# A last half query tile shared by two head pairs, and the k of some groups transposed by TensorE

## The chip, the core and the metric

The kernel runs on one core of a Trainium2 chip. The metric is the device time of one execution in microseconds (us). Before the change it is 247.95 us, the median of three runs (247.35 to 249.12).

## What is computed

Blockwise causal attention for 8 batches of 8 heads (576 tokens, head size 64), then a layer on its output: two matrices, the larger of the two results for each element, and a third matrix.

```
scores = scale * np.matmul(q, k.transpose(0, 1, 3, 2))
mask = block_i >= block_j            # blocks of 64 positions
attn = softmax(np.where(mask, scores, -1e9))
x = np.matmul(attn, v)               # then (B, S, H * D) as (4608, 512)
h1 = x @ w1                          # (4608, 1024)
h2 = x @ w2
out = np.maximum(h1, h2) @ w_out     # (4608, 512)
```

Inputs and output are float32; products run in bfloat16 with float32 sums.

## The kernel before

**Tiling.** A *pair* p (0 to 31, four to a batch) is two heads that lie one above the other on the 128 partitions of `qT` and `kT`. A *group* g (0 to 15, `NG`) is two pairs, p = 2g and 2g + 1. The 576 queries of a pair are four tiles of 128 (t = 0 to 3) and one of 64 (t = 4, `NCH - 1`). Keys lie in five chunks c in the same way.

**Getting q and k in.** `load_qk` fetches a group's q and k by one request each of 576 KB on SP's queue (after a small Pool memset that holds the request until the buffer is free); `cast` makes them bfloat16 on Pool; `transposes` turns them with 18 TensorE transposes into two PSUM tiles (`ps_m`), which VectorE and ScalarE copy to `qT` or `kT`. q takes this way in all groups. For k, `by_dma` says from g = 6 on (`T_DMA`) that it comes otherwise: `load_blocks` issues four smaller requests from Pool that cast on the way, and `transpose_blocks` issues two DMA transposes on SP's queue. `t_pair` runs the transposes of the next group, q's in even steps and k's in odd ones; `pad_keys` then copies a piece of k on Pool.

**Attention.** `tile_0`, `tile_1` and `tile_2` put a pair's scores (TensorE, `scores` and `corner_scores`, on 64 rows of the array each, for the two heads) into two PSUM tiles `ps_s`; ScalarE takes exp into `aT`; Pool's memsets cut the masked corners (`mask`). Two steps later (`LAG`) `av` multiplies them with v: `aT` is the stationary operand, v with a column of ones the moving one (65 columns), so that the last column is the sum of the row. For query tile t it takes t + 1 matmuls a head. `av` is called twice a pair, for t = 0, 1 and for t = 2, 3, 4; for t = 4 it takes 128 columns of `aT`, 64 of which belong to no query (the padding `APAD`). VectorE takes reciprocals and multiplies into `xp`, bfloat16, three buffers of a pool (`xpool`), each for a group. `xp` is transposed into `xT` by TensorE (`x_out`) for groups 0 to 3 and 15, and for the others by two DMA transposes on SP's queue (`x_dma`).

**The layer.** Its matmuls are generators (`h_unit`, `product` and others) which `fill(n)` advances by n matmuls of weight between the attention parts. A maximum is rewritten with a difference matrix (`d_sb`, `m_sb`), and products of the blocks are combined from sums. They use the same four PSUM banks (`ps_m`) as `av` and the transposes.

**Order.** The order on every engine is the order of the calls (`manual_schedule`). After a start written out by hand, a loop over g = 3 to 15 does for each of its two pairs: `fill`, `av` of the pair two steps back in its two calls with a short `fill` between them, the DMA transposes that are due, `t_pair`, the scores of two tiles, the copies out, the exps, and `pool_work`, which issues Pool's later loads (q and k of group g + 3, casts for g + 2, v of the next batch but one in pieces by `load_v`, k's blocks). What is left of the group's fill comes at its end. After the loop, pairs 30 and 31 get their `av`, then `x_out(15)`, and the rest of the layer runs.

Of the kernel before, what the change touches and what calls it, by code (L numbers as in the profile page):

```python
# [8 lines left out]
FP32 = mybir.dt.float32  # L9
BF16 = mybir.dt.bfloat16  # L10
# [4 lines left out]
def kernel(  # L15
# [10 lines left out]
    nc = tc.nc  # L26

    B, H, S, D = q.shape
    P = 128
    BLK = 64  # L30
    HP = H // 2
# [12 lines left out]
    RPP = S // NP  # L44
    NG = NPAIR // 2
# [4 lines left out]

    CB = [0, 448, 768, 960, 1024]
    AW = 1600
    APAD = 64
    NCH = 5


# [3 lines left out]
    def a_col(p, c, t):  # L60
        if p >= HP:
            return CB[c] + t * P
        late = t * P >= QCUT
        return t * P + {
            0: 384 - QCUT if late else 0, 1: 704 - QCUT if late else 256 - P,
            2: 1024 - QCUT, 3: 1408 - 3 * P, 4: 1344 - 4 * P,
        }[c]
# [12 lines left out]
    wpool = ctx.enter_context(tc.tile_pool(name="wpool", bufs=1))  # L80
    ring = ctx.enter_context(tc.tile_pool(name="ring", bufs=1))
    small = ctx.enter_context(tc.tile_pool(name="small", bufs=4))
    xpool = ctx.enter_context(tc.tile_pool(name="xp", bufs=3))
    raw = ctx.enter_context(tc.tile_pool(name="raw", bufs=3))
    wraw = ctx.enter_context(tc.tile_pool(name="wraw", bufs=4))
    qkn = ctx.enter_context(tc.tile_pool(name="qkn", bufs=2))
    g_pool = ctx.enter_context(tc.tile_pool(name="g", bufs=2))
    y_pool = ctx.enter_context(tc.tile_pool(name="y", bufs=6))
    ps_s = ctx.enter_context(tc.tile_pool(name="ps_s", bufs=2, space=bass.MemoryType.PSUM))
    ps_m = ctx.enter_context(tc.tile_pool(name="ps_m", bufs=4, space=bass.MemoryType.PSUM))  # L90
# [1 line left out]
    ctx.enter_context(tc.manual_schedule())  # L92


    NV, NA, NT = 3, 4, 4
    qT_r = [ring.tile([P, S], BF16, name=f"qT{r}") for r in range(NT)]
    kz_r = [ring.tile([P, 3 * BLK], BF16, name=f"kz{r}") for r in range(NT)]
    kT_r = [ring.tile([P, S], BF16, name=f"kT{r}") for r in range(NT)]
    vv_r = [ring.tile([P, NCH, H, D + 1], BF16, name=f"vv{r}") for r in range(NV)]
    aT_r = [ring.tile([P, 2, AW + APAD], BF16, name=f"aT{r}") for r in range(NA)]  # L100
    xT = ring.tile([P, NDM, NTOK + BLK], BF16, name="xT")
    d_sb = wpool.tile([P, NDM, d_ff], BF16, name="d_sb")
    bT_sb = wpool.tile([P, NFF, d_model], BF16, name="bT_sb")
# [6 lines left out]
    qk_n = {}  # L110
    dve, pool, act = nc.vector.tensor_copy, nc.gpsimd.tensor_copy, nc.scalar.copy

    def load_qk(g, queues, gated=False):
        b, u = divmod(g, GPB)
        for nm, src, queue in (("q", q, queues[0]), ("k", k, queues[1])):
            if queue is None or by_dma(nm, g):
                continue
            raws[nm, g] = t = raw.tile([P, 2, RPP * D], FP32, name=f"{nm}raw")
            if gated:
                nc.gpsimd.memset(t[:, 0, :1], 0.0)  # L120
            queue.dma_start(
                out=t[:],
                in_=src[b, 4 * u:4 * u + 4].rearrange(
                    "(s h) (p t) d -> (h p) s (t d)", h=2, t=RPP),
            )

    T_DMA = {nm: 6 for nm in "k"}
    blk_n = {}

    def by_dma(nm, g):  # L130
        return g >= T_DMA.get(nm, NG)

    def load_blocks(nm, g):
        b, u = divmod(g, GPB)
        blk_n[nm, g] = n = raw.tile([P, S // BLK, 2, D], BF16, name=f"{nm}b", tag=f"{nm}raw")
        for h in range(2):
            for s in range(2):
                nc.gpsimd.dma_start(  # L138
                    out=n[h * BLK:(h + 1) * BLK, :, s],
                    in_=(q if nm == "q" else k)[b, 4 * u + 2 * s + h].rearrange(  # L140
                        "(j p) d -> p j d", p=BLK),
                )
# [10 lines left out]
    def cast(nm, g, parts):  # L153
        if by_dma(nm, g):
            return
        t = raws[nm, g].rearrange("p s (t d) -> p t s d", d=D)
        if (nm, g) not in qk_n:
            qk_n[nm, g] = qkn.tile([P, RPP, 2, D], BF16, name=f"{nm}n")
        n = qk_n[nm, g]
        for copy, j0, j1 in parts:  # L160
            copy(out=n[:, j0:j1], in_=t[:, j0:j1])  # L161

    def load_v(b, c):
        rows = min(P, S - c * P)
        nc.gpsimd.dma_start(  # L165
            out=vv_r[b % NV][P - rows:, c, :, :D],
            in_=v[b, :, c * P:c * P + rows, :].rearrange("h p d -> p h d"),
        )
# [7 lines left out]
    for j in range(d_ff // WB):  # L176
        row, n = (1, j) if j < 3 else (3, 0)
# [17 lines left out]
    def load_wo(i):  # L195
        ds = slice(i * WH, (i + 1) * WH)
        nc.gpsimd.dma_start(out=wo_sb[:, :, ds], in_=wor[:, :, ds])
# [13 lines left out]
    for r in range(NV):  # L211
        nc.vector.memset(vv_r[r][:, :, :, D:D + 1], 1.0)
        nc.vector.memset(vv_r[r][:BLK, NCH - 1, :, :], 0.0)
    for r in range(NA):
        nc.vector.memset(aT_r[r][:, :, AW:], 0.0)
    for r in range(NT):
        nc.vector.memset(kz_r[r][:, BLK:2 * BLK], 0.0)
    cast("q", 0, ((dve, 0, 7), (pool, 7, RPP)))
# [276 lines left out]
    def fill(n):  # L495
        while n > 0:
            if not current:
                k = next((k for k, t in enumerate(todo) if t[2] <= done_tokens[0]), None)
                if k is None:
                    return max(0, n)  # L500
                current.append(todo.pop(k))
            t = current[0]
            next(t[1])
            n -= t[3]
            t[0] -= 1
            if not t[0]:
                current.pop()
        return 0
# [8 lines left out]
    xps = {}  # L517
# [68 lines left out]
    def burst_q1(p):  # L586
        burst(p, ((0, QCUT, 320), (1, QCUT, 192)), 384)

    def burst_q2(p):
        burst(p, ((1, 448, P), (2, QCUT, 320), (4, 512, BLK)), 896)  # L590

    def burst_q3(p):
        burst(p, ((3, 384, 192),), 1408)
# [11 lines left out]
    def tile_0(p):  # L605
        u = ps_s.tile([P, 2, 512], FP32, name="ps_s", tag="s")
        scores(p, u, 0, 0, 0, 512)
        return lambda: (exp(p, u, 512, 0), mask(p, 0))

    def tile_1(p):  # L610
        u = ps_s.tile([P, 2, 512], FP32, name="ps_s", tag="s")
        scores(p, u, 0, 0, 512, 64)
        scores(p, u, 64, 1, 128, 448)
        return lambda: (exp(p, u, 512, 512), mask(p, 576))
# [17 lines left out]
    def region(*tiles):  # L632
        for out in tiles:
            out()

    def av(p, ts):
        b, hp = divmod(p, HP)
        vv = vv_r[b % NV]
        a = aT_r[p % NA]
        n = len(ts)  # L640
        h0 = hp // 2 * 4 + hp % 2
        if p % 2 == 0 and ts[0] == 0:
            xps[p // 2] = xpool.tile([P, 2, NCH, 2, D], BF16, name="xp")
        xp = xps[p // 2]
        po = ps_m.tile([P, n, 2, D + 1], FP32, name="ps_o", tag="m")
        n_mm = 2 * sum(t + 1 for t in ts)
        mm = 0
        for gi, t in enumerate(ts):
            for hh in range(2):
                for c in range(t + 1):  # L650
                    a0 = a_col(p, c, t)
                    nc.tensor.matmul(  # L652
                        po[:, gi, hh, :], a[:, hh, a0:a0 + P], vv[:, c, h0 + 2 * hh, :],
                        start=(mm == 0), stop=(mm == n_mm - 1),
                    )
                    mm += 1
        rec = small.tile([P, 3, 2, 1], FP32, name="rec")
        nc.vector.reciprocal(rec[:, :n, :, 0], po[:, :, :, D])  # L658
        nc.vector.tensor_mul(  # L659
            xp[:, :, ts[0]:ts[0] + n, p % 2].rearrange("q s t d -> q t s d"), po[:, :, :, :D],  # L660
            rec[:, :n].to_broadcast([P, n, 2, D]),
        )

    def x_by_dma(g):
        return BY_DMA <= g < NG - 1
# [48 lines left out]
    def pool_work(s):  # L714
        g, i = divmod(s, 2)
        if s == 4:
            load_qk(4, (SP, SP), gated=True)
        elif s == 5:
            load_qk(5, (SP, SP), gated=True)
            cast("q", 4, ((pool, 0, RPP),))  # L720
            cast("k", 4, ((pool, 0, RPP),))
        else:
            if i == 1 and g + 3 < NG:
                load_qk(g + 3, (SP, SP), gated=True)
            if i == 1 and g + 2 < NG:
                cast("q", g + 2, ((pool, 0, RPP),))
                cast("k", g + 2, ((pool, 0, RPP),))
            nb, j = divmod(s + 2, HP)
            if nb < B:
                for c in ((0, 1), (2, 3, 4), (), ())[j]:  # L730
                    load_v(nb, c)
            for nm in "qk":
                if i == 1 and g + 3 < NG and by_dma(nm, g + 3):
                    load_blocks(nm, g + 3)
# [12 lines left out]
    def av_with(p, n):  # L747
        av(p, [0, 1])
        fill(n)
        av(p, [2, 3, 4])  # L750

    LOW = (0, -(-QCUT // RPP))
    HIGH = (LOW[1], NP)
# [55 lines left out]
    burst_q1(2)  # L809
    transposes("q", 2, (dve, act))()  # L810
    burst_q2(2)
    av(0, [2, 3, 4])
    burst_q3(2)
    masks_q(2)
    cast("k", 2, ((pool, 0, RPP),))
    load_wo(0)
    load_wo(1)
    av(1, [2, 3, 4])
    burst_q1(3)
    burst_q2(3)  # L820
    av(2, [2, 3, 4])
    transposes("k", 2, (dve, act))()
    burst_q3(3)
    masks_q(3)
# [6 lines left out]
    diff_w(1)  # L831
    fill(2)
    outs = tile_0(4), tile_1(4)
    av(3, [2, 3, 4])
    region(*outs)
    fill(2)
    diff_w(2)
# [10 lines left out]
    n = fill_of(GPB)  # L848
# [10 lines left out]
    for g in range(GPB + 1, NG):  # L859
        a, b = 2 * g, 2 * g + 1  # L860
# [3 lines left out]
        n, new = fill_of(g), done_tokens[0]  # L864
# [72 lines left out]
```

## Time and profile before

The profiled execution took 247.61 us, with a span of 245.8 us from its first to its last instruction. PE is TensorE's matmuls, PEld its weight loads (which overlap the matmuls), DVE is VectorE, ACT ScalarE, POOL GpSimd, SP the queue engine. "Idle" is time in which the engine waited just before such an instruction.

| what | count | mean ns | idle before it, us |
|---|---|---|---|
| weights for attention times v, 128x128 (L652) | 960 | 98 | 6.9 |
| products of the layer, 128x256, `sums` and `bT_sb` (L390) | 216 | 273 | 0.0 |
| exp of 128x1024 (ACT, L568) | 92 | 1023 | 31.1 |
| reciprocal of 4 columns (DVE, L658) | 32 | 177 | 1.8 |
| reciprocal of 6 columns (DVE, L658) | 32 | 192 | 5.0 |
| cast of q, 128x1152 (POOL, L161) | 14 | 1160 | 0.6 |
| Pool's DMA issue for k's blocks (L138) | 40 | 765 | 0.0 |
| Pool's DMA issue for v (L165) | 40 | 857 | 1.1 |

| request | queue | count | KB each | median us to landing |
|---|---|---|---|---|
| q | SP | 16 | 576 | 6.0 |
| k, large | SP | 5 | 576 | 7.4 |
| k, blocks | POOL | 40 | 72 | 6.8 |
| v | POOL | 32 | 128 | 7.3 |
| DMA transposes of k | SP | 20 | | 6.5 |
| DMA transposes of xp | SP | 22 | | 5.4 |

How to read it: a matmul's length is its time through the array, and matmuls follow one another before the earlier one is out, so what one costs is the distance between two starts. In a row of the groups by shape, "128*128" is the part of the array that is used, rows by columns; then come output and input shapes, the count, the busy time, the mean length and the idle time before.

### The profile page before, as it was taken

What the parts mean: (1) busy time and instruction counts of PE and PEld (TensorE: products, weight loads), DVE (VectorE), ACT (ScalarE), POOL (GpSimd) and SP (SyncE); (2) the same over time, 40 slices, a digit from 0 to 9 for tenths busy, and PEclk for the clock granted to TensorE, in tenths of its full rate; (3) what the DMA queues carried; (4) which work ended last, traced back from release to release, by engine and by line L of the source; (5) the groups of instructions that cost most, each with busy time, mean ns of one, the idle gap of its engine ahead of it and who ended that gap; (6) DMA issues with size and microseconds to landing.
All of it is one profiled execution on the core that took longest, in us unless ns stands there. A gap on an engine that the chain in (4) does not pass through costs nothing.

```text
span 245.8 us, 7595 instructions
## 1 busy us (share of the span) xinstructions
PE 234.4 (95%) x3093; PEld 167.3 (68%) x3109; DVE 185.4 (75%) x395; ACT 143.8 (58%) x200; POOL 129.6 (53%) x294
## 2 busy tenths in 40 slices
PE   7689899999999999999999999999999999999993
PEld 2347666688865886588558755875587578567782
DVE  4976989999677958795879587957785788526573
ACT  2888871677677748673867386748673730462200
POOL 1996952669959584948593859485621210010000
PEclk9999999999999999999999999999999999999998
DMA  6999999579999999999999999999994321301125
GB/s 233 318 206 306 231 278 195 172 137 188 153 196 180 168 163 222 184 201 183 244 227 130 208 164 272 122 223 193 134 138 97 100 39 45 131 0 43 47 86 172
DMA packets 108867, 41.33 MB, mean 168 GB/s; under 512 B 89248, under 2 KB 102688, under 8 KB 108832
## 3 DMA queue, kind: packets, MB, share of 16 engines
q0 software_dynamic: 65952, 11.87, 69.4%
q1 hardware_dynamic: 42464, 28.32, 51.7%
q10 hardware_dynamic: 416, 0.66, 0.8%
q8 instruction: 24, 0.39, 0.7%
q14 instruction: 11, 0.09, 0.1%
HBM read 34.60 MB, written 9.44 MB: 179 GB/s over the span
## 4 chain that ended last, share of the span: by engine, by line
PE 87%; DVE 7%; ACT 4%; issue 1%; ACTq 0%
PE ps_p L390 35%; PE ps_h L244 24%; PE ps_o L652 11%; PE ps_s L544 9%; PE ps_w L514 3%; ACT aT L568 3%; PE ps_qT L525 2%; DVE sums L358 2%; DVE sums L364 1%; DVE g L252 1%; DVE m_sb L277 1%; PE ps_s L562 1%; PE ps_xe L690 1%; PE ps_bT L261 1%; DVE qT L533 1%
## 5 line engine op out<-in xcount | busy, mean ns | idle before, releaser
L568 ACT ACTIVATE aT<-ps_s 128x1024 bf16<-128x1024 f32 (+2 forms) x100 | 95.7, 994 | 32.1 <-PE ps_s L544 24.0
L244 PE MATMUL ps_h<-xT,d_sb 128*128 128x512 bf16 (+3 forms) x307 | 68.0, 357 | 1.0 <-DVE d_sb L191 0.3
L573 POOL MEMSET aT<- 64x128 bf16 x124 | 21.8, 200 | 52.8 <-ACT aT L568 51.9
L244 PEld LDWEIGHTS <-d_sb 128*128 128x128 bf16 x320 | 29.7, 98 | 26.7 <-issue 2.2
L652 PEld LDWEIGHTS <-aT 128*128 128x128 bf16 x960 | 37.2, 98 | 6.9 <-issue 0.8
L652 PE MATMUL ps_o<-vv,aT 128*128 128x65 bf16 x960 | 39.8, 194 | 0.3 <-DVE xp L659 0.3
L250 ACT ACTIVATE g<-ps_h 128x512 bf16<-128x512 f32 (+1 forms) x40 | 23.3, 587 | 23.3 <-PE ps_h L244 22.3
L165 POOL DMA_DIRECT2D vv<-in_v_dram x40 | 33.9, 857 | 1.1 <-issue 0.9
L252 DVE TENSOR_SCALAR g<-ps_h 128x512 bf16<-128x512 f32 (+2 forms) x40 | 23.6, 594 | 13.1 <-PE ps_h L244 12.8
L659 DVE TENSOR_TENSOR xp<-ps_o,rec 128x256 bf16<-128x256 f32 (+1 forms) x64 | 31.4, 491 | 2.2
L544 PE MATMUL ps_s<-qT,kT 64*128 64x64 bf16 (+6 forms) x344 | 31.3, 280 | 1.8 <-ACT kT L533 0.7
L390 PE MATMUL ps_p<-sums,bT_sb 128*128 128x256 bf16 x216 | 32.8, 273 | 0.0
L390 PEld LDWEIGHTS <-bT_sb 128*128 128x128 bf16 x288 | 27.5, 98 | 4.5 <-issue 1.4
L138 POOL DMA_DIRECT2D kb<-in_k_dram x40 | 29.5, 765 | 0.0
L533 ACT COPY qT<-ps_qT 128x576 bf16<-128x576 bf16 (+1 forms) x17 | 10.3, 614 | 23.2 <-PE ps_qT L525 23.2
L390 PEld LDWEIGHTS <-g 128*128 128x128 bf16 x220 | 19.8, 98 | 4.8 <-issue 2.8
L390 PE MATMUL ps_p<-wo_sb,g 128*128 128x256 bf16 (+1 forms) x148 | 22.7, 270 | 0.0
L161 POOL CAST qn<-qraw 128x1152 bf16<-128x1152 f32 (+1 forms) x16 | 17.1, 1067 | 5.1 <-DMA qraw<-in_q_dram 5.1
L544 PEld LDWEIGHTS <-kT 64*128 64x128 bf16 x344 | 12.2, 94 | 10.5 <-issue 5.1
L658 DVE RECIPROCAL rec<-ps_o 128x4 f32<-128x4 f32 (+1 forms) x64 | 11.8, 184 | 6.8 <-PE ps_o L652 6.8
L236 POOL COPY g<-g 128x512 bf16<-128x512 bf16 x8 | 5.9, 733 | 20.6 <-ACT g L250 20.3
L364 DVE TENSOR_TENSOR bT_sb<-g 128x1024 bf16<-128x1024 bf16 x18 | 12.4, 688 | 5.4 <-ACT g L250 4.8
(90 smaller groups left out, 326.1 us busy)
## 6 DMA issues: line engine op xcount, KB each, us to landing
qraw<-in_q_dram SPq DMA_DIRECT2D x16, 576.0 KB, 6.0
out_dram<-y SPq DMA_DIRECT2D x35, 256.0 KB, 3.9
vv<-in_v_dram POOLq DMA_DIRECT2D x32, 128.0 KB, 7.3
kraw<-in_k_dram SPq DMA_DIRECT2D x5, 576.0 KB, 7.4
kb<-in_k_dram POOLq DMA_DIRECT2D x40, 72.0 KB, 6.8
w1raw<-in_moe_w_dram POOLq DMA_DIRECT2D x4, 512.0 KB, 8.8
xT<-in_moe_w_dram POOLq DMA_DIRECT2D x4, 256.0 KB, 9.2
wo_sb<-in_moe_w_out_dram POOLq DMA_DIRECT2D x2, 512.0 KB, 10.9
```

Source lines behind the costliest of these rows:

```text
L138: nc.gpsimd.dma_start(out=n[h * BLK:(h + 1) * BLK, :, s], in_=(q if nm == "q" else k)[b, 4 * u + 2 * s + h].rearrange("(j p) d -> p j d", ...
L161: copy(out=n[:, j0:j1], in_=t[:, j0:j1])
L165: nc.gpsimd.dma_start(out=vv_r[b % NV][P - rows:, c, :, :D], in_=v[b, :, c * P:c * P + rows, :].rearrange("h p d -> p h d"),)
L244: nc.tensor.matmul(pt[:, :w], d_sb[:, c, f * P:(f + 1) * P], xT[:, c, t0:t0 + w], start=(c == 0), stop=(c == NDM - 1),)
L250: nc.scalar.activation(out=g[:, f, m:m + w], in_=pt[:, :w], func=AF.Relu)
L252: nc.vector.tensor_scalar_max(g[:, f, m:m + w], pt[:, :w], 0.0)
L390: nc.tensor.matmul(pt[:, q0:q0 + w], lhs[c][:, s * P:(s + 1) * P], rhs[c][:, m:m + w], start=(c == 0 and q0 == 0), stop=(c == 5 and q0 + w ...
L544: nc.tensor.matmul(ps[:, hh, col:col + w], kT[r, k0:k0 + P], qT[r, q0:q0 + w], start=True, stop=True,)
L568: nc.scalar.activation(out=aT_r[p % NA][:, :, a0:a0 + w], in_=ps[:, :, :w], func=AF.Exp, scale=scale,)
L573: (eng or nc.gpsimd).memset(aT_r[p % NA][BLK:, :, a0:a0 + BLK], 0.0)
L652: nc.tensor.matmul(po[:, gi, hh, :], a[:, hh, a0:a0 + P], vv[:, c, h0 + 2 * hh, :], start=(mm == 0), stop=(mm == n_mm - 1),)
L659: nc.vector.tensor_mul(xp[:, :, ts[0]:ts[0] + n, p % 2].rearrange("q s t d -> q t s d"), po[:, :, :, :D], rec[:, :n].to_broadcast([P, n, 2 ...
```

## The change

1. `av` for an even pair covers t = 0 to 3 alone. For an odd pair its second call covers t = 2, 3 and then t = 4 of both pairs of the group (`rest`): 64 columns of `aT` as the stationary operand, so that one head's output lies on the lower and the other's on the upper 64 partitions of the PSUM tile, the two heads alternating. The number of matmuls stays. VectorE multiplies these two halves by two instructions of 64 partitions each into the lower 64 partitions of `xp`.
2. `xp` becomes a ring of two fixed buffers (three before), whose upper half of tile 4 is set to zero at the start. The padding of `aT` and its memsets are gone.
3. `by_dma` now holds for odd groups alone: k of groups 6, 8, 10, 12 and 14 comes by `load_qk`, `cast` and `transposes`; for groups 8 to 14 the cast goes to a buffer of its own (`klate`). Groups 7, 9, 11, 13 and 15 keep Pool's blocks and the DMA transposes.
4. `pool_work` issues v's five chunks as 3, 1, 1 and 0 over four steps (2, 3, 0, 0 before).

```
     def by_dma(nm, g):
-        return g >= T_DMA.get(nm, NG)
+        return g >= T_DMA.get(nm, NG) and g % 2 > 0
...
         if (nm, g) not in qk_n:
-            qk_n[nm, g] = qkn.tile([P, RPP, 2, D], BF16, name=f"{nm}n")
+            if nm == "k" and g > T_DMA["k"]:
+                qk_n[nm, g] = klate.tile([P, RPP, 2, D], BF16, name="kl")
+            else:
+                qk_n[nm, g] = qkn.tile([P, RPP, 2, D], BF16, name=f"{nm}n")
...
     def av(p, ts):
...
+            xps[g] = xp_r[g % NX]
+        xp = xps[g]
+        rest = p % 2 and ts[0] > 0
+        n = 4 + 2 * rest
+        po = ps_m.tile([P, n, D + 1], FP32, name="ps_o", tag="m")
+        parts = [(po[:, 2 * gi + hh, :], p, hh, c, t, P)
+                 for gi, t in enumerate(ts) for hh in range(2) for c in range(t + 1)]
+        if rest:
+            parts += [(po[hh * BLK:(hh + 1) * BLK, 4 + i, :], p - 1 + i, hh, c, NCH - 1, BLK)
+                      for i in range(2) for c in range(NCH) for hh in range(2)]
+        for mm, (o, pp, hh, c, t, w) in enumerate(parts):
+            a0 = a_col(pp, c, t)
+            h0 = pp % HP // 2 * 4 + pp % 2
+            nc.tensor.matmul(
+                o, aT_r[pp % NA][:, hh, a0:a0 + w], vv[:, c, h0 + 2 * hh, :],
+                start=(mm == 0), stop=(mm >= len(parts) - 1 - rest),
+            )
+        rec = small.tile([P, 6, 1], FP32, name="rec")
+        nc.vector.reciprocal(rec[:, :n, 0], po[:, :, D])
         nc.vector.tensor_mul(
...
+            po[:, :4, :D].rearrange("q (t s) d -> q t s d", s=2),
+            rec[:, :4].rearrange("q (t s) d -> q t s d", s=2).to_broadcast([P, 2, 2, D]),
         )
+        if rest:
+            for s in range(2):
+                r = slice(s * BLK, (s + 1) * BLK)
+                nc.vector.tensor_mul(
+                    xp[:BLK, s, NCH - 1], po[r, 4:, :D], rec[r, 4:].to_broadcast([BLK, 2, D]))
...
-                for c in ((0, 1), (2, 3, 4), (), ())[j]:
+                for c in ((0, 1, 2), (3,), (4,), ())[j]:
                     load_v(nb, c)
...
-        av(p, [2, 3, 4])
+        av(p, [2, 3])
```

More of the change, by code (lines that the diff above doesn't have):

```diff
@@ L52 @@
     AW = 1600
-    APAD = 64
     NCH = 5
@@ L82 @@
     small = ctx.enter_context(tc.tile_pool(name="small", bufs=4))
-    xpool = ctx.enter_context(tc.tile_pool(name="xp", bufs=3))
     raw = ctx.enter_context(tc.tile_pool(name="raw", bufs=3))
@@ L86 @@
     qkn = ctx.enter_context(tc.tile_pool(name="qkn", bufs=2))
+    klate = ctx.enter_context(tc.tile_pool(name="kl", bufs=1))
     g_pool = ctx.enter_context(tc.tile_pool(name="g", bufs=2))
@@ L92 @@
     ctx.enter_context(tc.manual_schedule())
-    NV, NA, NT = 3, 4, 4
+    NV, NA, NT, NX = 3, 4, 4, 2
     qT_r = [ring.tile([P, S], BF16, name=f"qT{r}") for r in range(NT)]
@@ L99 @@
     vv_r = [ring.tile([P, NCH, H, D + 1], BF16, name=f"vv{r}") for r in range(NV)]
-    aT_r = [ring.tile([P, 2, AW + APAD], BF16, name=f"aT{r}") for r in range(NA)]
+    aT_r = [ring.tile([P, 2, AW], BF16, name=f"aT{r}") for r in range(NA)]
+    xp_r = [ring.tile([P, 2, NCH, 2, D], BF16, name=f"xp{r}") for r in range(NX)]
     xT = ring.tile([P, NDM, NTOK + BLK], BF16, name="xT")
@@ L125, in load_qk @@
             )
-    T_DMA = {nm: 6 for nm in "k"}
+    T_DMA = {"k": 6}
     blk_n = {}
     def by_dma(nm, g):
-        return g >= T_DMA.get(nm, NG)
+        return g >= T_DMA.get(nm, NG) and g % 2 > 0
     def load_blocks(nm, g):
@@ L213 @@
         nc.vector.memset(vv_r[r][:BLK, NCH - 1, :, :], 0.0)
-    for r in range(NA):
-        nc.vector.memset(aT_r[r][:, :, AW:], 0.0)
+    for r in range(NX):
+        nc.vector.memset(xp_r[r][BLK:, :, NCH - 1], 0.0)
     for r in range(NT):
@@ L637, in av @@
         b, hp = divmod(p, HP)
+        g = p // 2
         vv = vv_r[b % NV]
-        a = aT_r[p % NA]
-        n = len(ts)
-        h0 = hp // 2 * 4 + hp % 2
         if p % 2 == 0 and ts[0] == 0:
[L643 to L656, printed above, removed]
@@ L657, in av @@
-        rec = small.tile([P, 3, 2, 1], FP32, name="rec")
-        nc.vector.reciprocal(rec[:, :n, :, 0], po[:, :, :, D])
+            xps[g] = xp_r[g % NX]
[8 more added lines that the diff above has]
+                      for i in range(2) for c in range(NCH) for hh in range(2)]
@@ L659, in av @@
+        for mm, (o, pp, hh, c, t, w) in enumerate(parts):
[7 more added lines that the diff above has]
+        nc.vector.reciprocal(rec[:, :n, 0], po[:, :, D])
         nc.vector.tensor_mul(
-            xp[:, :, ts[0]:ts[0] + n, p % 2].rearrange("q s t d -> q t s d"), po[:, :, :, :D],
@@ L661, in av @@
-            rec[:, :n].to_broadcast([P, n, 2, D]),
-        )
+            xp[:, :, ts[0]:ts[0] + 2, p % 2].rearrange("q s t d -> q t s d"),
+            po[:, :4, :D].rearrange("q (t s) d -> q t s d", s=2),
+            rec[:, :4].rearrange("q (t s) d -> q t s d", s=2).to_broadcast([P, 2, 2, D]),
+        )
+        if rest:
[3 more added lines that the diff above has]
+                    xp[:BLK, s, NCH - 1], po[r, 4:, :D], rec[r, 4:].to_broadcast([BLK, 2, D]))
@@ L811 @@
     burst_q2(2)
-    av(0, [2, 3, 4])
+    av(0, [2, 3])
     burst_q3(2)
@@ L817 @@
     load_wo(1)
-    av(1, [2, 3, 4])
+    av(1, [2, 3])
     burst_q1(3)
     burst_q2(3)
-    av(2, [2, 3, 4])
+    av(2, [2, 3])
     transposes("k", 2, (dve, act))()
@@ L833 @@
     outs = tile_0(4), tile_1(4)
-    av(3, [2, 3, 4])
+    av(3, [2, 3])
     region(*outs)
```

## Prediction

> **What bounds the kernel now.** I read the page's busy table first, then the chain of waits in order of time, the busy time by stretch, the waits of each engine, the timeline of one group, and the groups by shape.
>
> The busy table and the head of the chain, then busy time by stretch (length, then busy us and instructions of PE, PEld, DVE, ACT, POOL, then clock, DMA share, GB/s):
>
> ```profile
> PE 234.4 (95%) x3093; PEld 167.3 (68%) x3109; DVE 185.4 (75%) x395; ACT 143.8 (58%) x200; POOL 129.6 (53%) x294
> ...
> PE 87%; DVE 7%; ACT 4%; issue 1%; ACTq 0%
> ```
>
> ```profile
> 24.00:34.00 10.00, 8.67 (x155) 6.66 (x151) 9.60 (x20) 8.88 (x12) 8.74 (x20) 1.00 1.32 250
> 34.00:52.00 18.00, 17.16 (x258) 12.94 (x256) 17.16 (x39) 7.99 (x12) 7.46 (x18) 1.00 1.20 205
> 60.00:200.00 140.00, 139.33 (x1870) 98.34 (x1879) 106.59 (x221) 93.42 (x127) 87.49 (x209) 1.00 1.57 174
> ```
>
> From 60 us on TensorE is busy 139.33 of 140 us at full clock, and the list of PE's waits in that stretch is empty: nothing there makes TensorE wait for a DMA, for Pool, for VectorE. The stage ends when TensorE has issued its list, so an edit there is worth what it adds to or takes from that list, and nothing else unless it makes a new wait. Before 52 us VectorE matters too: it is busy 9.60 of 10 us, then 17.16 of 18, and the chain runs through it:
>
> ```profile
> 45.05 1.03 DVE sums L358 x2
> 46.54 0.42 DVE xp L659
> 47.33 1.12 DVE sums L358
> 48.59 0.57 DVE xp L659
> 49.56 0.66 PE ps_M L272 x6
> ```
>
> From 49.56 us on it is TensorE's almost without a break. What Pool and the DMA queues carry is off the path: the only late wait for k's transposed blocks is Pool's own, 1.1 us in two places.
>
> ```profile
> POOL kz L551 <- DMA kT<-kb: 1.1, 2, 0.7
> ```
>
> **The prices on TensorE**, from the timeline of one even step (start, length, engine, what). A length ends with the last matmul's pipeline, so a pitch is (length - one matmul) / (count - 1).
>
> ```profile
> 100.70 1.90 PE L244 MATMUL ps_h<-xT,d_sb 128*128 128x512 bf16 x8
> ...
> 103.27 0.89 PE L652 MATMUL ps_o<-vv,aT 128*128 128x65 bf16 x24
> ...
> 104.08 0.44 PE L525 MATMUL ps_qT<-ident,qn 64*128 64x64 bf16 x18
> ...
> 104.36 0.22 PE L562 MATMUL ps_s<-qT,kz 64*128 64x64 bf16 x4
> ...
> 104.42 0.57 PE L544 MATMUL ps_s<-qT,kT 64*128 64x320 bf16 x6
> ...
> 104.92 0.39 PE L390 MATMUL ps_p<-wo_sb,g 128*128 128x256 bf16 x2
> ```
>
> ```profile
> L652 PE MATMUL ps_o<-vv,aT 128*128 128x65 bf16 x960 | 39.8, 194 | 0.3 <-DVE xp L659 0.3
> L659 DVE TENSOR_TENSOR xp<-ps_o,rec 128x384 bf16<-128x384 f32 x32 | 17.9, 558 | 1.1
> L659 DVE TENSOR_TENSOR xp<-ps_o,rec 128x256 bf16<-128x256 f32 x32 | 13.6, 424 | 1.1
> L533 DVE COPY qT<-ps_qT 128x576 bf16<-128x576 bf16 x15 | 11.2, 749 | 0.2 <-PE ps_qT L525 0.2
> L533 ACT COPY qT<-ps_qT 128x576 bf16<-128x576 bf16 x15 | 9.6, 639 | 23.2 <-PE ps_qT L525 23.2
> ```
>
> An attention matmul (128x65, whole array) costs (0.89 - 0.194) / 23 = 30.3 ns. Eighteen transposes on half arrays take from 104.08 to 104.36, 0.28 us less the 0.01 of the first one's late start, so 0.27 us: two, one on each half of the rows, pass in about 30 ns. Going from the whole array to half arrays costs: the last attention matmul starts at 103.27 + 0.70 = 103.97, the first transpose at 104.08, so 0.11 - 0.03 = 0.08 to 0.09 us. Going back: the 320-to-512 column scores end at 104.99, their last 512-column pair started 0.38 earlier at 104.61, the next product starts at 104.92: 0.31, of which a 512-column matmul takes (1.90 - 0.38) / 7 = 0.217, so 0.093. I take 0.09 for any change of array shape.
>
> **The change, part by part.** *The last half tile.* A group's two pairs spend 2 x 10 whole-array matmuls on query tile 4, half of it padding: 20 x 30.3 = 0.61 us. After, the odd pair issues 20 matmuls with 64 weight columns, alternately for the lower and upper 64 output partitions. Same count; the gain is only in whether two pass together. No row here has a 128-row, 64-column matmul. The nearest is the half-array transpose, whose pairs pass in 30 ns; by it the tile costs 10 x 30.3 = 0.30 us, a gain of 0.30. The other end is no overlap at all, 0.61 us, and above that a weight load that isn't hidden (a rival). I take 0.30, as the split into two independent halves is the same in kind.
>
> Against it stand new changes of array shape. For pairs 5, 7, ... 29 transposes or scores follow, which changed shape already, so one is added each: 13 x 0.09. Pair 31 is followed by whole-array work: two. Together 15 x 0.09 = 1.35 us. Groups 2 to 15 (14 of them) run where TensorE is the bound: 14 x 0.30 = 4.2 us gained. Net -2.9.
>
> *VectorE for it.* Per group before: twice 177 + 424 + 192 + 558 = 2.70 us (reciprocals of 4 and 6 columns, multiplies). After: three times 601, then 192 + 424 and two multiplies of 64x128. The step from 256 to 384 columns is 134 ns, so each is 424 - 134 = 290: 3.00 us. The 0.30 us more hides after 60 us, where VectorE has 33 of 140 us free; if that cover went, 14 x 0.30 = 4.2 us. Groups 0 and 1 fall where it is saturated: up to +0.6 us there, against 0.56 us of slack at 34.7 us and less TensorE work; the even pair 4 on the chain even gains 0.13. I book +0.2, bounds -0.4 and +0.8.
>
> *k of groups 6, 8, 10, 12, 14.* Removed: per group four Pool DMA issues (0.77 us each, 3.1 us), four 72 KB loads, two DMA transposes on SP's queue. Added: one 576 KB load on SP, a 0.1 us memset and a 1.16 us cast on Pool, 18 transposes, a 0.75 us copy on VectorE and a 0.64 us copy on ScalarE. Nothing of the removed work is on the path, so it gains nothing. The transposes are: 5 x 0.27 = +1.35 us. They come between half-tile matmuls and scores, with no further change of shape. ScalarE does its copy ahead of two exps; those feed attention two steps later, and ScalarE has 46 of 140 us free; uncovered it is 3.2 us. VectorE's is a rival below.
>
> *Load order of v, ring of two for xp, memsets.* v's chunks 2, 3, 4 are issued at most a step later, still two steps before use; Pool issues as many. An xp buffer is rewritten two groups after it was filled, over 12 us after its DMA transpose was issued, which lands in 5.4. Nothing, or, if a landing were late, a VectorE wait behind which PSUM evictions queue; SP's queue has fewer transposes, so less likely than now. The startup memsets are 0.2 us shorter in VectorE's wait for the first load: 0.
>
> Sum: -2.9 + 0.2 + 1.35 = -1.3 us. The profiled execution took 247.61, so 246.3; the median of the runs is 0.34 higher: 246.6.
>
> The Trainium skill speaks against it: its page "TensorEngine Tiling (Array Packing)", section Feature Incompatibilities, says that column tiling excludes Fast Weight Load. The page "TensorE: Matmul & The Clock Gate", section LDWEIGHTS, gives columns / 1.2 ns for a plain load, an estimated 53 ns for 64 columns. If each half loads its own, that gives 53 per pair, about 10 x 53 = 0.53 us a group and a sum near +1.8; one after the other, 20 x 53 = 1.06 us and a sum near +10. No row here shows a 64-column load.
>
> **The rivals.** (1) *The halves don't pass together*: weights for one half are loaded only after those of the other, so each matmul still takes 30 ns. For it: only row halves are seen to overlap here, and every load in the trace has 128 columns. Then nothing is gained, and -1.3 becomes +2.9 (+0.2 for the early groups): 247.95 + 3.1 = 251.1, slower. The point from which it decides: the 2.9 us of cost are met by a pitch of 30.3 - 2.9 / (14 x 20) = 20 ns a matmul; above that the change loses, and from 29 ns on it loses over 1%. (2) *Loads of 64 columns lie open*: one row's load lasts 98 ns; open once a pair it is 49 a matmul, 16 x 20 x 0.0187 = +6.0, plus 1.35 + 1.35 + 0.4: 257. Against it: all loads are hidden now. (Here and in rival 1 the two outcomes of the Trainium skill's rule are worked out from rows.) (3) *PSUM*: in odd steps the two transpose banks and the attention bank, three of four, now wait on 0.43 + 0.75 = 1.2 us more of VectorE, and TensorE's next unit waits for a bank. If all of it shows in five groups, +5.9: 252.5; half, 249.5. Against: even steps do the same for q, with no wait after 60 us. (4) *More than the sum*: halves at no cost of switching, 245.2.
>
> **How the numbers follow.** Forecast 246.6 with chance 0.45 (its own range 245.6 to 248); rival 1 0.27, with any pitch from 20 to 30 ns; rival 2 0.13; rival 3 0.10; rival 4 0.05. Range 245.3 to 252.6: from rival 4 to rival 3's full price; left out are rival 2 and half of 4, some 0.16. One per cent is 2.5 us, about what a measurement of this kernel can tell from no change: faster below 245.5, slower above 250.4. Faster: rival 4 and a little of the forecast, 0.06. Same: the forecast, the lower part of rival 1 (0.09) and of 3 (0.04), 0.57. Slower: the rest, 0.37.
>
> **What would show it.** In the groups by shape a 128*64 row of 320 matmuls; in the timeline, 20 of them starting within 0.3 us (forecast) or 0.6 and more (rivals 1, 2). About 0.09 us on each side of them. PE's waits after 60 us still empty; an entry naming a copy of k or xp is rival 3. k's transposes at 0.27 us in five odd steps. Wrong outright: if TensorE got faster or slower outside these places, or if the removed DMA work shortened anything.

## The result and the profile after

After the change the kernel takes 248.62 us (median of 20 runs, 248.17 to 249.45), beside 247.88 us for the kernel before in the same session (20 runs, 247.12 to 251.82). The ratio is 1.0033 [1.0017, 1.0049]: 0.8 us slower. Here and below, ratios leave out executions that took over 1.5% longer than the fastest of their kernel. The change costs time where the forecast was a gain of 1.3 us, though it stays inside the range that was stated. The profiled execution took 248.82 us with a span of 247.0, so it is compared with before's 247.61 and 245.8.

The busy table and the head of the chain, then the busy time by the same three stretches, of the kernel after:

```profile
PE 234.9 (95%) x3199; PEld 165.8 (67%) x3199; DVE 194.5 (79%) x430; ACT 146.6 (59%) x205; POOL 121.0 (49%) x284
...
PE 82%; DVE 10%; ACT 2%; DMA 2%; issue 1%; POOL 1%; DVEq 0%; POOLq 0%
```

```profile
24.00:34.00 10.00, 8.42 (x154) 6.50 (x155) 9.52 (x21) 8.51 (x12) 8.78 (x20) 1.00 1.31 250
34.00:52.00 18.00, 17.20 (x261) 12.79 (x259) 17.15 (x40) 8.24 (x12) 7.29 (x18) 1.00 1.13 202
60.00:200.00 140.00, 140.00 (x1991) 97.94 (x1989) 114.64 (x250) 96.27 (x133) 79.34 (x196) 1.00 1.19 174
```

TensorE is still the bound from 60 us on (140.00 of 140), and the trace has 1991 matmuls there instead of 1870. Of the 121 more, 90 are k's transposes; some others are records that before's trace lacks (it has 307 of 320 for `ps_h`). VectorE carries 8 us more in that stretch and has room for it. Before 52 us VectorE is as full as it was, and the chain's share on VectorE rose from 7 to 10%. Two waits of TensorE before 60 us are new (in total, times, longest):

```profile
PE ps_qT L528 <- DVE y L422: 0.3, 1, 0.3
PE ps_o L660 <- DVE y L418: 0.3, 1, 0.3
```

They stand in the chain behind VectorE's new multiplies (L674). In before's chain VectorE's work ended at 49.16 us; in after's it goes on to 57.84:

```profile
51.80 0.27 DVE xp L674
52.07 0.01 issue
52.08 0.29 DVE xp L674
...
57.23 0.61 DVE y L422
```

The attention matmuls of after, by shape (count, then busy us, mean ns, idle before):

```profile
L660 PE MATMUL ps_o<-vv,aT 128*128 128x65 bf16 x640 | 30.0, 194 | 0.6 <-DVE y L418 0.3 <-DVE xp L666 0.3
L660 PE MATMUL ps_o<-vv,aT 128*64 128x65 bf16 x320 | 8.1, 198 | 0.0
L660 PEld LDWEIGHTS <-aT 128*64 128x64 bf16 x320 | 6.3, 111 | 0.8
L660 PEld LDWEIGHTS <-aT 128*128 128x128 bf16 x640 | 27.4, 98 | 7.2 <-issue 1.3 <-DVE xp L666 0.6 <-DVE aT L576 0.2
L674 DVE TENSOR_TENSOR xp<-ps_o,rec 64x128 bf16<-64x128 f32 x32 | 9.0, 282 | 0.4
```

The 128*64 row exists, with 320 matmuls. Its busy time needs care: two matmuls that run at the same time are counted once. By their starts, two halves begin 0 to 7 ns apart and the next two 23 to 33 ns later, but 49 ns later after the first two of a step. Twenty take about 0.345 us, 34.7 ns a pair (32 without the first), where the whole-array form took 0.606. So the halves do pass together, and a group gains 0.26 us. The weight loads of 64 columns last longer than those of 128, 111 against 98 ns, and remain hidden.

What went the other way is seen in one even step. First the chain in order of time (start, length), after and then before:

```profile
66.83 0.18 PE ps_o L660 x6
67.02 0.66 PE ps_p L393 x6
67.67 0.42 PE ps_o L660 x14
68.09 0.51 PE ps_qT L528 x18
68.60 0.06 PE ps_s L565 x4
```

```profile
66.24 0.18 PE ps_o L652 x6
66.42 0.66 PE ps_p L390 x6
67.08 0.72 PE ps_o L652 x24
67.80 0.37 PE ps_qT L525 x18
68.17 0.06 PE ps_s L562 x4
```

The second call of `av` shrank from 24 matmuls (0.72 us) to 14 (0.42), as it should. But q's transposes behind it grew from 0.37 to 0.51. The timeline of after there (start, length, engine) names the cause:

```profile
67.51 0.59 PE L660 MATMUL ps_o<-vv,aT 128*128 128x65 bf16 x14
...
67.69 0.42 DVE L666 TENSOR_TENSOR xp<-ps_o,rec 128x256 bf16<-128x256 f32 x1
68.02 0.46 PEld L528 LDWEIGHTS <-qn 64*128 64x128 bf16 x18
68.03 0.57 PE L528 MATMUL ps_qT<-ident,qn 64*128 64x64 bf16 x18
```

The multiply of the *first* call's PSUM tile ends at 67.69 + 0.42 = 68.11 us. The transposes go to two PSUM tiles in turn. The first starts at 68.03 into a free bank; the second needs the bank which that multiply is reading. It starts at 68.17, 0.06 us after the multiply ends, and all others stand behind it. TensorE loses 0.11 us. Before, ten more matmuls lay in between and covered it. The same stall, 0.110 to 0.113 us each, is at 92.36, 116.68, 141.01 and 165.33 us, five in all. Each is too short to appear in the list of waits, which is why that list still looks empty past 60 us.

At the other end of the kernel, SP's waits from 240 us on, after and then before (in total, times, longest):

```profile
SPq L945 <- DMA out_dram<-y: 1.9, 1, 1.9
```

```profile
SPq L932 <- DMA out_dram<-y: 1.4, 3, 0.6
```

SP ends the program by waiting for its outstanding stores. Its requests signal on eight semaphores in turn, and the closing waits take the semaphores in fixed order. k's move takes five requests off SP's queue (ten DMA transposes fewer, five loads more), which shifts the turn: the last store to land now has the semaphore that is waited for first, and SP still has to pass seven further waits of about 0.06 us after it. Before, most were passed while the last store was under way. From the last data packet of a store to the end of the span it is 2.26 us after and 1.72 before. The turn explains only a part of that, as the runs below show.

### The profile page after: what moved, and what is told of

The parts are those of the page before. It is cut to its first block, busy times and chain, and to the rows that moved or that the text cites. A ratio compares the mean times of both kernels' runs of the same rounds, so it can differ in the third digit from the quotient of the medians.

```text
span 247.0 us, 7819 instructions
## 1 busy us (share of the span) xinstructions
PE 234.9 (95%) x3199; PEld 165.8 (67%) x3199; DVE 194.5 (79%) x430; ACT 146.6 (59%) x205; POOL 121.0 (49%) x284
## 4 chain that ended last, share of the span: by engine, by line
PE 82%; DVE 10%; ACT 2%; DMA 2%; issue 1%; POOL 1%; DVEq 0%; POOLq 0%
PE ps_p L393 33%; PE ps_h L247 24%; PE ps_o L660 9%; PE ps_s L547 8%; PE ps_qT L528 2%; DMA qraw<-in_q_dram 2%; DVE sums L361 2%; PE ps_kT L528 1%; PE ps_w L517 1%; ACT aT L571 1%; DVE sums L367 1%; DVE d_sb L194 1%; DVE m_sb L280 1%; DVE g L255 1%; PE ps_s L565 1%
## 5 line engine op out<-in xcount | busy, mean ns | idle before, releaser
L247 PE MATMUL ps_h<-xT,d_sb 128*128 128x512 bf16 (+3 forms) x320 | 69.4, 358 | 0.5 <-DVE d_sb L194 0.5
L576 POOL MEMSET aT<- 64x128 bf16 x124 | 22.3, 200 | 63.7 <-ACT aT L571 61.2
L660 PEld LDWEIGHTS <-aT 128*128 128x128 bf16 (+1 forms) x960 | 33.7, 102 | 8.1 <-issue 1.3
L660 PE MATMUL ps_o<-vv,aT 128*128 128x65 bf16 (+1 forms) x960 | 37.0, 195 | 0.6 <-DVE y L418 0.3
L666 DVE TENSOR_TENSOR xp<-ps_o,rec 128x256 bf16<-128x256 f32 x64 | 27.2, 425 | 2.2
L665 DVE RECIPROCAL rec<-ps_o 128x4 f32<-128x4 f32 x64 | 11.6, 180 | 5.2 <-PE ps_o L660 5.0
L138 POOL DMA_DIRECT2D kb<-in_k_dram x20 | 14.6, 745 | 0.0
```

Source lines behind the costliest of these rows:

```text
L247: nc.tensor.matmul(pt[:, :w], d_sb[:, c, f * P:(f + 1) * P], xT[:, c, t0:t0 + w], start=(c == 0), stop=(c == NDM - 1),)
L576: (eng or nc.gpsimd).memset(aT_r[p % NA][BLK:, :, a0:a0 + BLK], 0.0)
L660: nc.tensor.matmul(o, aT_r[pp % NA][:, hh, a0:a0 + w], vv[:, c, h0 + 2 * hh, :], start=(mm == 0), stop=(mm >= len(parts) - 1 - rest),)
L666: nc.vector.tensor_mul(xp[:, :, ts[0]:ts[0] + 2, p % 2].rearrange("q s t d -> q t s d"), po[:, :4, :D].rearrange("q (t s) d -> q t s d", s=2),
```

## The experiments

Each kernel is the kernel after with the edit shown, unless said otherwise. Times are medians (range, number of runs), the ratio is to the kernel before on the same chip in the same batch, whose medians were 248.07 (e1 to e4), 247.71 (a1, a2, e6, e7) and 248.12 us (a3, b1, e8).

| kernel | what | us | ratio [95%] |
|---|---|---|---|
| e1 | half tile alone | 246.68 (246.0 to 253.0, 10) | 0.9926 [0.9895, 0.9956] |
| e2 | k alone | 249.36 (248.4 to 250.18, 12) | 1.0055 [1.003, 1.008] |
| e3 | halves not alternating | 249.49 (248.9 to 250.19, 10) | 1.0063 [1.0041, 1.0086] |
| e4 | one more change of shape | 250.25 (249.8 to 251.14, 6) | 1.0095 [1.0063, 1.0127] |
| a1 | early groups as before | 248.31 (248.1 to 249.17, 9) | 1.0035 [1.0019, 1.0051] |
| a2 | one unit of fill moved ahead | 247.89 (247.42 to 249.29, 12) | 1.0017 [0.9999, 1.0035] |
| e6 | e1 and a2 | 245.9 (245.19 to 247.28, 6) | 0.993 [0.9902, 0.9957] |
| e7 | e1, a1 and a2 | 248.43 (245.46 to 250.67, 12) | 0.9953 [0.991, 0.9995] |
| a3 | q's late loads split in two | 247.89 (247.56 to 248.68, 12) | 0.9979 [0.9943, 1.0016] |
| b1 | a1, a2 and a3 | 247.24 (246.94 to 247.94, 12) | 0.9955 [0.9926, 0.9985] |
| e8 | e6 again | 248.7 (245.66 to 250.33, 12) | 0.999 [0.9941, 1.004] |

**The two parts of the change, each alone.** In e1 k comes by Pool's blocks and DMA transposes as before:

```
-        return g >= T_DMA.get(nm, NG) and g % 2 > 0
+        return g >= T_DMA.get(nm, NG)
```

> The changed kernel, with k of all groups from 6 on again by Pool's blocks and DMA transposes. My theory: k's 18 transposes cost TensorE 0.27 us in each of five groups and the work they replace was free, so 1.35 us go: about 247.2, a ratio to the kernel before of 0.9975 (0.995 to 0.999). The waits of 0.11 us in q's transposes in five even steps may stay. Rival A, the relief of Pool and the DMA queues pays for the transposes: no better than the changed kernel, 248.6 (1.003). Rival B, the shared half tile gains nothing on the whole, and all of the loss is k's: 247.9 minus nothing, ratio 1.000.

Measured 0.9926: the half tile alone is a gain of 1.8 us by the ratio, 1.1 to 2.6 by its interval. That is three times the 0.6 us expected. In the trace it ends 2.0 us before after does, 1.2 of them on TensorE and 0.8 behind the last data packet (1.48 us in place of 2.26). e2 is the kernel before with the other half of the change:

```
     def by_dma(nm, g):
-        return g >= T_DMA.get(nm, NG)
+        return g >= T_DMA.get(nm, NG) and g % 2 > 0
...
+            if nm == "k" and g > T_DMA["k"]:
+                qk_n[nm, g] = klate.tile([P, RPP, 2, D], BF16, name="kl")
...
-    xpool = ctx.enter_context(tc.tile_pool(name="xp", bufs=3))
+    xpool = ctx.enter_context(tc.tile_pool(name="xp", bufs=2))
```

> The kernel before with only the move of k in groups 6, 8, 10, 12 and 14 to the large request, cast and TensorE transposes (xp has two buffers instead of three, since the extra k buffer takes the space). My theory: 5 x 0.27 = +1.35 us on TensorE, 249.2, ratio 1.0055, with no wait of TensorE after 60 us. Rival A (the relief pays): 247.9, ratio 1.000. A third possibility, two xp buffers are too few: VectorE waits for a DMA at the first multiply of a group, and the time is above 250.

Measured 1.0055. Laid beside before's trace instruction by instruction, TensorE falls behind by 0.27 to 0.33 us in each of the five odd steps and by 1.4 in all by 231 us. So the loss of the whole change sits with k, and the half tile's gain pays for part of it. The two ratios together would give 0.998 where 1.0033 was measured, 1.3 us more. Some 0.7 of that is at the end: the span goes on past the last data packet of a store for 1.48 us in e1, 1.79 in e2 and 2.26 in after, against 1.72 in before.

**Do the halves pass together because they alternate?** In e3 all five chunks of one head come before those of the other:

```
-                      for i in range(2) for c in range(NCH) for hh in range(2)]
+                      for i in range(2) for hh in range(2) for c in range(NCH)]
...
-                start=(mm == 0), stop=(mm >= len(parts) - 1 - rest),
+                start=(mm == 0), stop=(mm == len(parts) - 1 or bool(rest) and mm == len(parts) - 6),
```

> The changed kernel with the 20 matmuls of the half tile in the order of one head's five chunks, then the other's, so that neighbours go to the same half of the columns. My theory: the overlap of the two halves comes from the alternation; without it a matmul costs at least the 30 ns of a 65-column pass, the tile 0.6 us or more instead of 0.345, at least 14 x 0.26 = +3.6 us: 252.2 or more, ratio to the kernel before 1.017 or more. If the weight loads of 64 columns then lie open, 50 ns a matmul and 258. Rival: TensorE's queue finds the partner by itself, nothing changes, 248.6, ratio 1.003.

The expectation missed. Twenty matmuls took 0.37 us in place of 0.31 (both counted without the last one's own length), 0.06 us a step, and still overlapped, at 19 ns from start to start where whole-array ones take 30. Since one head's five go to the same half, the overlapping ones must stand several instructions apart in the program; which half a start belongs to isn't seen in the trace. By its ratio against that of after the kernel lost some 0.7 us.

**What does a change of shape cost?** e4 puts the half tile between tiles 2 and 3, so that the array changes to 64 columns, back to 128, and then to the transposes:

```
+            parts = parts[:6] + parts[14:] + parts[6:14]
...
-                start=(mm == 0), stop=(mm >= len(parts) - 1 - rest),
+                start=(mm == 0), stop=(mm == len(parts) - 1),
```

> The changed kernel with the half tile's 20 matmuls put between query tiles 2 and 3 of the odd pair, so that one more change of the array's shape falls into each odd step (3 instead of 2), with the same matmuls. My theory: a change costs 0.095 us wherever it stands: 13 x 0.095 = +1.2 us, 249.85, ratio to the kernel before 1.008. Rival: the 0.095 us seen beside the half tile are the pipeline's length at the end of a run, not a cost of changing: no difference, 248.6, ratio 1.003.

Measured 1.0095 against 1.0033, in the trace 0.11 us an odd step more: 99 ns for 128*64 to 128*128, 96 for 128*128 to 64*128, in the place of one change of that size. The price of a change stands.

**The early groups.** a1 gives groups 0 to 3 the attention of before (two calls of 10 and 24 matmuls, padded `aT`), where VectorE is full:

```
+        if g < 4:
+            if ts[0]:
+                ts = [2, 3, 4]
...
+            nc.vector.tensor_mul(
+                xp[:, :, ts[0]:ts[0] + n, p % 2].rearrange("q s t d -> q t s d"), po[:, :, :, :D],
+                rec[:, :n].to_broadcast([P, n, 2, D]),
+            )
+            return
```

> The changed kernel, but with the attention of before (tile 4 of each pair by 128 columns, one multiply of 384 columns on VectorE) in groups 0 to 3, the ones that fall before 62 us. My theory: there VectorE is the bound, and its 0.30 us more a group set the time, not TensorE; the changed kernel stood 0.6 us behind the one before at 62 us, so 0.5 to 0.6 us go: 248.1, ratio to the kernel before 1.0005 to 1.001. Rival: the 0.6 us come from the order of the start (memsets, the other buffers) or from TensorE's changes of shape: then at most the 4 x 0.1 us of shape changes go and the tile's gain with them, no difference, 1.003.

By the trace it stands 0.48 us ahead of after at 62 us and stays there, but 0.41 of that it has at 38 us already. There the traces of all kernels lie between 0.55 us ahead of before's and 0.61 behind, whatever their early groups do. The times show nothing: 1.0035 against after's 1.0033.

Laid beside before's trace score by score, the traces do show where the early groups cost time. Between before's scores of 54 us and those of 57 us TensorE falls behind by 0.42 to 0.55 us in all eight kernels with the new form in the early groups (after, e1, e3, e4, e6, e8, a2, a3), at the two waits shown above, and by nothing in the four with the old form (e2, e7, a1, b1). That is groups 2 and 3; the prediction expected it in groups 0 and 1. But a1 and b1 lose 0.28 us again from 57 to 60 us. From 38 to 62 us after falls behind by 0.34 us in all and a1 by 0.28, so that this remedy had next to nothing to bring.

**The stall of q's transposes.** a2 moves one unit of layer work, of the same group, ahead of the shortened second call:

```
+        more = int(g % 2 and g > 4)
...
-            av_with(p - LAG, lo)
+            av_with(p - LAG, lo + (p == a) * more)
...
-        fill(n - 2 * (lo + hi))
+        fill(n - 2 * (lo + hi) - more)
```

> The changed kernel, with one unit more of the layer's matmuls (0.22 us) moved from the end of each odd group from 5 on to between the two calls of the even pair's attention; the same matmuls in another order. My theory: the second PSUM tile of q's transposes waits 0.11 us in those steps for VectorE's multiply of the first call, since the even pair's second call is 10 matmuls (0.3 us) shorter and no longer covers it; with 0.22 us more between them the wait goes: 5 x 0.11 = -0.55 us, 248.1, ratio 1.001. Rival: the wait moves to the next PSUM tile, and nothing changes: 1.003.

All five stalls are gone. The chain of a2 in the step shown above:

```profile
66.59 0.18 PE ps_o L660 x6
66.77 0.88 PE ps_p L393 x8
67.64 0.42 PE ps_o L660 x14
68.06 0.37 PE ps_qT L528 x18
```

Eight products in place of six lie between the two calls (the other two are missing later), and q's transposes are back at 0.37 us. From 62 to 231 us the kernel gains 0.64 us on after, against 5 x 0.11 = 0.55, and the ratio falls from 1.0033 to 1.0017.

**The closing waits.** a3 issues the q of groups 11 to 15 as two requests each. That adds five requests to SP's queue and so turns the semaphores back; the data and the matmuls are the same:

```
+            if nm == "q" and g in range(11, 16):
+                for s in range(2):
+                    queue.dma_start(
+                        out=t[:, s],
...
```

> The changed kernel, with the q loads of groups 11 to 15 as two requests of 288 KB each. SP's requests use eight completion semaphores in turn; moving k takes five requests off SP, so that the last store ends on the semaphore that the closing list waits for first, with eight more waits of about 0.06 us behind it. Five more requests put it back on the sixth, as in the kernel before. My theory: the end comes 0.5 us sooner, from 2.26 us after the last store's landing to about 1.7: 248.1, ratio 1.001; nothing changes before 240 us. Rival: the closing list takes the same time in any order: 248.6, ratio 1.003.

SP's closing wait is no longer one of 1.9 us, and the span ends 1.70 us after the last data packet of a store (2.26 in after):

```profile
SPq L953 <- DMA out_dram<-y: 1.3, 2, 0.7
```

The median is 247.89, with 248.12 for before in that batch. The interval of the ratio, 0.9943 to 1.0016, is wide and touches after's lower end, so the 0.5 us rest on the trace more than on the times.

The expectation's mechanism is only a part of it. e2 has the same turn as after and the same wait of 1.9 us, yet its span ends 1.34 us after the semaphore of its last store, where after needs 1.80 and e1, with the turn of before, 1.05. So the turn costs about 0.3 us, five more waits of 0.06. The rest of after's delay is mainly a gap of 0.35 us between two of SP's last instructions (245.77 to 246.12 us). e3, e4, a1 and a2 have it too, e2 and e1 don't. In a3 and b1 a gap of that length lies ahead of the last waits, and mostly overlaps the last store. What the gap is, no run shows.

**The tile and the moved unit without k.** e6 is e1 with a2's edit, e7 has a1's as well; b1 has the three remedies with k still on TensorE; e8 is e6 once more.

> The half tile alone (k by Pool's blocks from group 6 on), with the same shift of fill in odd groups. My theory: 0.55 us less than the half tile alone, which had a ratio of 0.9926 (246.7): 246.1, ratio 0.990 to 0.991. Its one wait of 0.1 us for a transpose of xp by DMA at 166 us may come back, and more than once, as TensorE gets earlier. Rival as in the run with k: no difference.

> The half tile alone, with the shift of fill and with the attention of before in groups 0 to 3: the candidate for a version faster than both. My theory: -0.55 and -0.5 us on the half tile alone (246.7): 245.6, ratio to the kernel before 0.988 to 0.990. If the early loss isn't VectorE's, no better than the run with the shift alone.

> The changed kernel with all three: attention of before in groups 0 to 3, a unit more of fill ahead of the even pair's second call in odd groups, and five split q loads. It keeps k of every second late group on TensorE. My theory: -0.25, -0.75 and -0.5 us on 248.5: 247.0, ratio to the kernel before 0.996 to 0.998, so that the half tile's gain and k's price are left. A second thing: the kernel with the half tile, old early attention and more fill, but k by DMA, ran either at 245.5 to 246 or at 248.3 to 250.7, with TensorE waiting for transposes of xp by DMA. If k's blocks and DMA transposes crowd those, this kernel has no such waits and its runs lie within 1.5 us. Rival: the late transposes come from TensorE being early; then they show here too, and runs above 249 appear.

> The half tile alone with a unit more of fill ahead in odd groups, once more for a closer ratio: 245.5 to 246, ratio 0.991 to 0.994. If late transposes of xp strike it as they struck the one with old early attention, some runs lie above 248.

e6's median came out as expected, 245.9. Its ratio, 0.993, is no lower than e1's, though by the traces it gains 0.8 us on e1 from 62 to 231 us. e7 did not come out: its runs spread from 245.46 to 250.67. e8, the same kernel as e6, had a median of 248.7 on another chip. TensorE's waits past 60 us for another engine or a DMA tell why (in total, times, longest), for e7, then e8, then b1:

```profile
PE ps_h L249 <- DMA xT<-xp: 2.3, 3, 1.5
```

```profile
PE ps_h L247 <- DMA xT<-xp: 3.0, 4, 2.0
```

```profile
PE ps_kT L538 <- DVE xp L679: 0.2, 1, 0.2
```

The layer's matmuls wait for the DMA transposes of xp. e6's profiled execution, a quick one of 245.57 us, has no such wait. In e8's chain one of them, issued at 160.67 us, is on the path for 8.75 us. The median landings, of e8, of after, and of b1:

```profile
xT<-xp SPq DMA_TRANSPOSE x22, 7.8
```

```profile
xT<-xp SPq DMA_TRANSPOSE x22, 3.7
```

```profile
xT<-xp SPq DMA_TRANSPOSE x22, 3.9
```

With all of k by DMA from group 6 on, xp's transposes take 6.0 to 7.8 us (e1, e6, e7, e8; 5.4 in the kernel before). With half of k moved to TensorE they take 3.6 to 4.7, in every kernel profiled, and TensorE waits for none of them past 60 us. a2 and e8 differ in k alone. So k's move buys what the prediction said it couldn't: it keeps xp's transposes on time when TensorE runs earlier.

The spread of the times points the same way, with and without the half tile. In the eight kernels with half of the late groups' k on TensorE (e2 among them, which has no half tile) the runs of each, 93 in all, lie within 1.0 to 1.9 us of each other; before's spread over 4.7 to 5.4 us in every batch. No trace of a late run of before was kept, so that late transposes are its reason too is not shown. Whether the shorter landing is due to ten DMA transposes fewer or to twenty block loads fewer wasn't tried.

b1 gives the best of both: 247.24 us in a spread of 1.0 us, ratio 0.9955 [0.9926, 0.9985], with k on TensorE, no wait of TensorE for a DMA past 60 us, and 1.66 us from the last data packet to the end. It is faster than the kernel before by 0.15 to 0.74%, and than the kernel after. e6's 245.19 shows what the tile could reach if xp's transposes were always in time.

## Why the prediction was wrong, step by step

| term | predicted, us | measured, us | from |
|---|---|---|---|
| half tile, with its changes of shape | -2.9 | -1.9 | 12 x 0.26 gained, 13 x 0.097 paid |
| VectorE in the early groups | +0.2 | about +0.35 | after's trace from 38 to 62 us |
| k's transposes | +1.35 | +1.3 | 5 x 0.265 |
| q's transposes waiting | 0 | +0.55 | 5 x 0.11 |
| SP's end of the program | 0 | +0.5 | 2.26 - 1.72; some 0.3 by the turn |
| sum | -1.3 | +0.8 | times: +0.74 by the medians |

Of the 2.1 us between the two sums, the half tile's size makes 1.0, the stalls of q's transposes 0.55 and the end of the program 0.5. That the sum comes within 0.1 us of the times is in part luck: up to 38 us the traces alone differ by up to 0.6 us from before's.

- **The step whose reasoning failed is the cover of the even step.** The prediction looked for a PSUM wait in odd steps, behind VectorE's added work, and set against it that "even steps do the same for q, with no wait after 60 us". But that cover was itself part of what the change removed: the even pair's second call lost ten matmuls, 0.30 us, and it was these that hid the first call's multiply: five stalls of 0.11 us. Rival 3 had the mechanism (TensorE stands for a bank which VectorE still reads), but in the wrong step and from added work rather than removed cover. a2 shows it: move a unit into the gap, and the stall is gone.
- **The term that was most mis-sized is the tile, -1.9 us for -2.9.** The forecast's mechanism held, the halves pass together, and rivals 1 and 2 are ruled out. But a pair of halves takes 34.7 ns and not the transposes' 30, and only groups 4 to 15 run where TensorE is the bound. Groups 2 and 3 were counted in, since before's chain is TensorE's from 49 us on. The change itself moved that border: VectorE's added work keeps the chain until 57.84 us.
- **The end of the program was left out.** That k's move takes five requests off SP's queue was booked at nothing. It changed which semaphore the last store signals, and with the gap named above it cost 0.5 us at the far end of the kernel. SP's list of waits in before's trace shows such closing waits behind the last matmul. a3's trace supports the part of the turn.
- **"Nothing of the removed work is on the path, so it gains nothing"** was right for the trace of before and for the sum. It was incomplete for the design: e7 and e8 show that, once TensorE runs earlier, the removed DMA work would lie in the way.
- **Right:** 0.09 us for a change of shape (0.092 to 0.099 for the new kinds), 0.27 us for k's eighteen transposes (in e2, without the half tile, 0.27 to 0.33 a step), no wait for their copies by VectorE or ScalarE in the profile past 60 us. The load order of v and the two buffers of xp were not tried apart from the rest; in after's trace no wait of TensorE past 60 us names them.
- **The rule that spoke against it.** The rows show 34.7 ns a pair, with loads of 64 columns that last 111 ns and lie open nowhere. The estimated 53 ns a pair, which the prediction worked out from the Trainium skill's "TensorE: Matmul & The Clock Gate", section LDWEIGHTS, for halves that have no Fast Weight Load ("TensorEngine Tiling (Array Packing)", section Feature Incompatibilities), did not come: 320 loads of 111 ns would be 35.5 us in a row and kept the load path busy for 6.3, so they overlapped one another. Whether Fast Weight Load was in use is not seen in a trace.

## What to carry to other kernels

When a change takes matmuls out of TensorE's list, look at what they were covering: for each PSUM bank that TensorE writes soon after, compare its reader's end with the new start, also where the stall is too short for a list of waits. A saving counts only in the stretch where its engine is the bound, so mark the borders of that stretch before multiplying by the number of groups. An engine's added work can move such a border. Work that is off the path now may come onto it when the bound moves; judge a trade of TensorE time for DMA relief by the margin of each landing and the spread of the times, not by the present path alone.

## What the runs showed of the chip

- Matmuls on the two column halves of the array pass together also when they are issued five of one and then five of the other: 0.06 us more for twenty (e3).
- A load of 64 weight columns lasted 111 ns, one of 128 columns 98 ns; both stayed hidden behind matmuls.
- A pair of 64-column matmuls costs 34.7 ns against 30 for two transposes on the row halves or one matmul of the whole array; without the first pair after a change of shape, which took 52 ns, it is 32.
- A change of array shape costs 0.09 to 0.1 us between neighbouring matmuls (after, e4).
- The order of SP's closing waits against the turn of its semaphores moved the end of the kernel by 0.3 us (1.34 us from the last store's semaphore in e2, 1.05 in e1).
- The same 22 DMA transposes landed in 3.6 to 4.7 us (medians of a kernel) with half of k's late groups on TensorE, and in 5.4 to 7.8 us with all of these groups' k by DMA.
